# The low parts of a transform's operands on one engine, and two products of an MLP ahead of a layer

## The chip, the cores and the metric

The kernel runs on one core of a Trainium2 chip. The metric is the device time of one execution in microseconds (us). One launch takes eight float32 inputs and writes a float32 output of 2048 x 576.

## The reference

A token-mixing Fourier layer and an MLP read the same normalised input, and both are added to the input:

```python
xn = layernorm(x)                       # x: 2048 x 576
a  = xn @ dft_hid_re.T                  # first transform, along the 576 columns
b  = xn @ dft_hid_im.T
y  = dft_seq_re @ a - dft_seq_im @ b    # second transform, along the 2048 rows
h  = relu(xn @ w1)                      # w1: 576 x 4608
out = x + y + h @ w2                    # w2: 4608 x 576
```

The DFT matrices are inputs like the weights; no structure of theirs is used.

## The kernel before

**Numbers.** Every matrix product is made with float16 operands that come in two parts: a high part (the value rounded to float16) and a low part (the value less its high part, again in float16). A product is the sum of high x high, high x low and low x high. To make a split operand costs one rounding and one subtraction; the products themselves are blocked two by two and follow a scheme with seven multiplications, so that sums and differences of blocks are split as well.

**The engines' parts.** TensorE (PE in the profile) makes the products in float32 accumulators (PSUM). ScalarE (ACT) rounds and copies, VectorE (DVE) subtracts, adds and reduces, GpSimd (POOL) reduces over partitions, issues the DMAs that add results to a buffer `spill` in DRAM, and makes some subtractions. SyncE (SP) issues the loads and the transposing DMAs. Each engine works through its own instructions in the order in which the program lists them; the lists are written out by hand, as sequences of steps with names. `pinned(f)` issues the instructions of a step behind all that were issued before on PE, ACT and DVE.

**Stages.** The MLP runs over 9 blocks b of 512 columns of `w1`, and in each over 4 groups g of 512 rows of x; a step n is one pair (b, g). In step n, TensorE makes layer 1 of (b, g) and, between its parts, the seven products (0 to 6) of layer 2 of the step before, `mlp2_mm` (line L703). Layer 1 of block 0 is made by `mlp1_step` (L392 for the full depth of 128, L417 for the remaining 64 columns). The results of the products are read out of PSUM by `mlp2_out`: products 0, 2, 3 and 6 by a copy on ScalarE (L718), products 1, 4 and 5 by an add on VectorE (L722). Two PSUM buffers serve the products, so a product that starts a new buffer waits for an earlier read-out.

In block 0 the input is still being prepared. For group 3, four tiles are normalised (L306, L307), split (L313, L316) and transposed by four DMAs that SyncE issues (`transposes_dma`, L330). The first part of layer 1 of step 3, (0, 3), is the first reader of what these four transposes write. The steps 3 to 7 follow the sequence written out in the diff: `layer` is a part of layer 1, `m` a product of layer 2, `out2` its read-out, `slot`, `t_sum`, `then` and `count` are chores and read-outs that stand at that place when there are any (in step 3 the places "a" and "b" and the two `then`s hold nothing).

**The first transform.** It follows the MLP, in 8 steps s (two for each group). In a step TensorE makes seven products P1 to P7 for each half e of the columns (`dproduct`, L1429), in accumulators U0, U1, V and W. `take` reads them out, to a buffer X in float32: as copies on ScalarE (L1465) or as adds on VectorE (L1463). The take "u" for e = 1 is an add on VectorE that reads U1. Behind it `drests` (L1445), short matmuls over the remaining 64 columns, write U0, U1, W and V anew, so they can only begin when these have been read.

`convert(s, k)` makes, from a finished half of X, the seven split operands that the second transform reads. Its pieces have names:

- h1, h2, h3a, h3b: high parts, on ScalarE (L1476)
- l1, l2, l3a, l3b: low parts, `tensor_tensor` subtractions at L1480; l3a and l3b cover 128 x 576 each, and so does l1; l2 covers 128 x 288
- t13, t2, t4: differences of blocks in place, on VectorE (L1484, L1492, L1493)

`convert(s, 1)` ("one") is begun in step s itself and ended in step s + 1, where its end has the name "old"; `convert(s, 0)` ("two") is wholly made in step s + 1, under the name "late". So each of the steps 1 to 7 has two l3a and two l3b. Their order within a step, from the hand-written sequence, with the takes between them:

```python
("old", "t4"), ("old", "l3b"), ("old", "h3a"), ("late", "l1"), ("late", "h2"), (P5, 0), ("old", "l3a"), ("late", "l2"),
...
("c22", None), (P6, 1), ("r21", 1), ("late", "h3b"), ("late", "h3a"), (P7, 0), ("u", 0),
("late", "l3b"), (P3, 0), (P7, 1), ("u", 1), ("late", "l3a"), ("m", 0),
(P3, 1), ("rest", 0), ("w", None), ...
```

Before the change, l3a and l3b go to GpSimd in the steps 1 to 6 and to VectorE in step 7: a list `late_r` is empty until step 7 begins.

**The second transform** (`product`, L1644, with read-out at L1652) follows, with the split operands of `cre` and `cim` made on ScalarE and VectorE (L229, L230).

Of the kernel before, what the change touches and what calls it, by code (L numbers as in the profile page):

```python
# [54 lines left out]
def kernel(  # L55
# [17 lines left out]
    nc = tc.nc  # L73
# [611 lines left out]
    def mlp2(b, g, n):  # L685
        mlp2_mm(b, g, n)
        mlp2_out(b, g, n)
# [362 lines left out]
    def pinned(f, *a):  # L1050

        traced = nc.cur_bb.bb.instructions
        n = len(traced)
        with ExitStack() as s:
            for i in tails.values():
                s.enter_context(tc.issue_after(i))
            f(*a)
        for i in traced[n:]:
            if i.engine in ENGINES:
                tails[i.engine] = i  # L1060
# [187 lines left out]
    for n in range(2, len(steps)):  # L1248
        b, g = steps[n]
# [13 lines left out]
        if b >= BB:  # L1263
# [4 lines left out]
            then = lambda k: pinned(pend.pop(k)) if k in pend else None  # L1268
            m = lambda q: pinned(mlp2_mm, pb, pg, q)
            out2 = lambda q: pinned(mlp2_out, pb, pg, q)  # L1270
            slot = lambda k: [pinned(f) for f in chores.pop((g, k), ())]
            count = lambda q: pinned(passes.pop(0)) if passes else None
            more = lambda q: g % 2 and count(q)
            t_sum = lambda q: n == BB * NG and pinned(next, tq, None)
# [16 lines left out]
        if n > 2:  # L1291
            if n == 3:
                pend = {}
            psn = []
            m = lambda q: pinned(mlp2_mm, pb, pg, q)
            out2 = lambda q: pinned(mlp2_out, pb, pg, q)
            then = lambda k: pinned(pend.pop(k)) if k in pend else None
            layer = lambda i: pinned(mlp1_step, b, g, i, psn)
            now = lambda ks: [pinned(pairs[-1][k]) for k in ks.split()]
            pair = lambda i: pairs.append(pair_out(b, g, i, *psn[2 * i : 2 * i + 2]))  # L1300
            slot = lambda k: [pinned(f) for f in chores.pop((g, k), ())] if b else [pinned(work) for _ in range(WORK[k])]
            t_sum = lambda q: [pinned(next, tq, None) for _ in range(int(TS[n][q]))]
            count = lambda q: pinned(passes.pop(0)) if (n, q) > (6, 0) else None
            pairs = []
            for do, q in (
                (layer, 0), (then, "out6"), (slot, "a"), (then, "hS"), (t_sum, 0), (then, "lS"), (m, 0), (out2, 0),
                (slot, "b"), (t_sum, 1), (m, 1), (out2, 1), (slot, "c"), (t_sum, 2), (layer, 1), (count, 0),
                (t_sum, 3), (pair, 0), (now, "r hA hB lA s3 s1 s2 lB s4"), (m, 2), (out2, 2), (t_sum, 4),
                (m, 3), (out2, 3), (now, "hS"), (t_sum, 5), (now, "lS"), (slot, "d"), (layer, 2), (slot, "e"), (t_sum, 6),
                (m, 4), (out2, 4), (slot, "f"), (t_sum, 7), (m, 5), (out2, 5), (slot, "g"), (t_sum, 8), (count, 1),  # L1310
                (layer, 3), (pair, 1), (now, "r hA hB lA s3 s1 s2 lB s4"), (t_sum, 9), (slot, "h"), (m, 6),
            ):
                do(q)
            pend = {k: pairs[1][k] for k in ("hS", "lS")}
            pend["out6"] = lambda b=pb, g=pg: mlp2_out(b, g, 6)
            continue
# [147 lines left out]
        else:  # L1464
            order["da"] = nc.scalar.activation(dst, src, AF.Copy, scale=SCALE).ins  # L1465

    late_r = []

    def convert(s, k):

        g, c = divmod(s, 2)
        x, r = X[s % 2][:, k], R[g * TG + 2 * k + c]
        tt = nc.vector.tensor_tensor

        def hi(a, b):
            nc.scalar.activation(r[:, 0, a], x[:, b], AF.Copy)  # L1476

        def lo(a, b):
            tt = (nc.gpsimd if a.start > 2 and not late_r else nc.vector).tensor_tensor
            tt(r[:, 1, a], x[:, b], r[:, 0, a], ALU.subtract)  # L1480

        def t13():
            pair = x.rearrange("p (a b) e -> p a b e", b=2)[:, :, 0]
            tt(pair, x[:, 2:], pair, ALU.subtract)  # L1484

        return {
            "h1": lambda: hi(slice(0, 2), slice(0, 2)),
            "l1": lambda: lo(slice(0, 2), slice(0, 2)),
            "h2": lambda: hi(slice(2, 3), slice(3, 4)),
            "l2": lambda: lo(slice(2, 3), slice(3, 4)),  # L1490
            "t13": t13,
            "t2": lambda: tt(x[:, 3], x[:, 3], x[:, 0], ALU.subtract),  # L1492
            "t4": lambda: tt(x[:, 1], x[:, 1], x[:, 3], ALU.subtract),  # L1493
            "h3b": lambda: hi(slice(5, 7), slice(2, 4)),
            "l3b": lambda: lo(slice(5, 7), slice(2, 4)),
            "h3a": lambda: hi(slice(3, 5), slice(0, 2)),
            "l3a": lambda: lo(slice(3, 5), slice(0, 2)),
        }
# [52 lines left out]
    for s in range(NS):  # L1551
        lows = [(s, 0, P4), (s, 0, P3), (s, 1, P4), (s, 1, P3)]
        lows += [(s, e, P2) for e in range(2)]
        if s + 1 < NS:
            lows += [(s + 1, e, P5) for e in range(2)]
        end = s == NS - 1
        if end:
            late_r.append(True)
        one, two = convert(s, 1), convert(s, 0)
        if s == 0:  # L1560
            seq = (
                (P1, 0), ("pend", "out6"), ("pend", "s42"), ("c11", 0), ("pend", "hi1"), ("pend", "lo0"),
                 ("mlp", 0), ("pend", "lo1"),
                (P5, 0), ("c22", 0), ("mlp", 1), ("tail", 0), (P6, 0), ("r21", 0), ("mlp", 2), ("tail", 0),
                (P7, 0), ("u", 0), ("mlp", 3), ("tail", 0), (P3, 0), ("mlp", 4), ("tail", 0),
                (P1, 1), ("c11", 1), ("mlp", 5), ("tail", 0), (P5, 1), ("c22", 1), ("mlp", 6),
                (P6, 1), ("r21", 1), (P4, 0), (P7, 1), ("u", 1), ("open", 0), (P3, 1), ("rest", 0),
                ("c21", 0), ("w", None),
                ("one", "h1"), ("one", "l1"), ("one", "h2"), ("one", "l2"),
                (P4, 1), ("c21", 1), ("one", "t13"), ("one", "t2"),  # L1570
                (P2, 0), (P2, 1), ("v", None), ("one", "h3b"),
            )
        else:
            seq = (
                (P1, 0), ("c11", 0), ("late", "h1"), (P1, 1), ("c11", 1), ("old", "t4"), ("old", "l3b"),
                ("old", "h3a"), ("late", "l1"), ("late", "h2"), (P5, 0), ("old", "l3a"), ("late", "l2"),
                ("late", "t13"), (P6, 0), ("r21", 0), ("late", "t2"), ("late", "t4"), (P5, 1),
                ("c22", None), (P6, 1), ("r21", 1), ("late", "h3b"), ("late", "h3a"), (P7, 0), ("u", 0),
                ("late", "l3b"), (P3, 0), (P7, 1), ("u", 1), ("late", "l3a"), ("m", 0),
                (P3, 1), ("rest", 0), ("w", None), ("m", 1), ("m", 2), (P4, 0), ("c21", 0), ("one", "h1"),  # L1580
                ("one", "l1"), (P4, 1), ("c21", 1), ("one", "h2"), ("one", "l2"), ("one", "t13"), ("one", "t2"),
                (P2, 0), (P2, 1), ("v", None), ("one", "h3b"),
            )
        for what, e in seq:
            if what in ("old", "late", "one"):
                d = {"old": old, "late": late, "one": one}[what]
                if e in d and not (end and what == "one"):
                    pinned(d.pop(e))
            elif what == "pend":
                pinned(pend.pop(e))  # L1590
            elif what == "mlp":
                pinned(lambda: mlp2(*steps[-1], e))
            elif what == "tail":
                pinned(tail.pop(0))
            elif what == "open":
                ps2.release()
                psv = accumulators(("V", 2), ("W1", 2), side="left")
            elif what == "rest":
                pinned(lambda: drests(lows))
            elif what == "m":  # L1600
                if end:
                    pinned((lambda: operand(0), lambda: operand(1), lambda: addends(2))[e])
            elif isinstance(what, str):
                pinned(lambda: take(s, what, e))
            else:
                pinned(lambda: dproduct(s, e, what))
        old, late = one, two
        if s == 0:
            load_c(0, [0])
        if s == 3:  # L1610
            pinned(lambda: next(scale_c, None))
        if s == 5:
            load_c(0, [2, 3, 1])
# [47 lines left out]
    for n, (p, kh) in enumerate(units):  # L1661
# [7 lines left out]
        for i, (q, rq, first, row, col) in enumerate(PRODUCTS):  # L1669
            m = n * 7 + i  # L1670
# [73 lines left out]
```

## Time and profile before

| what | us |
|---|---|
| median of 3 runs | 1223.71 (1222.91 to 1224.64) |
| the profiled execution | 1222.8 |
| its span in the profile | 1221.0 |
| TensorE busy | 1208.1 |
| VectorE busy | 1005.6 |
| ScalarE busy | 720.2 |
| GpSimd busy | 192.5 |

The span runs from the first to the last instruction of the program; the execution's own time has 1.8 us around it. Busy times overlap, engine by engine. A row of the timeline has its start, its length, the engine, the line, the operation, what it writes and reads, and how many instructions in a row it stands for; in brackets the idle time of the engine before it and who ended that.

### The profile page before, as it was taken

How to read it: one execution, taken by the hardware profiler on the slowest of the kernel's cores; microseconds unless marked ns; L12 is line 12 of the kernel's file. 1: busy time of each engine (PE TensorE's matmuls, PEld its weight loads, DVE VectorE, ACT ScalarE, POOL GpSimd, SP SyncE). 2: the span in 40 equal slices, each digit the busy share in tenths (PEclk: the TensorE clock that was granted, in tenths of full speed). 3: DMA queues.
4: the chain of work that ended last, by engine and by line, in shares of the span. 5: the costliest groups of instructions: out<-in, count | busy, mean ns of one | idle time of the engine just before them, and what ended most of it. 6: DMA issues, size and time to landing. Idle time of an engine off the chain costs nothing.

```text
span 1221.0 us, 24573 instructions
## 1 busy us (share of the span) xinstructions
PE 1208.1 (99%) x10173; PEld 956.4 (78%) x10173; DVE 1005.6 (82%) x1623; ACT 720.2 (59%) x1077; POOL 192.5 (16%) x229
## 2 busy tenths in 40 slices
PE   8999999999999999999999999999999999999998
PEld 7656567888888888888888888877777777777776
DVE  9998998887797788788877977667898978787875
ACT  5646565866676776767666767555644433433342
POOL 2431211111121211111111211144300000000000
PEclk9999999999999999999999999999999999999999
DMA  9995645767666676667676667520165254534320
GB/s 320 210 156 87 104 73 136 154 136 162 157 133 168 132 180 127 142 151 153 136 164 157 126 160 158 94 30 1 62 205 179 72 185 137 177 108 147 100 89 20
DMA packets 84063, 164.64 MB, mean 135 GB/s; under 512 B 22640, under 2 KB 43632, under 8 KB 83952
## 3 DMA queue, kind: packets, MB, share of 16 engines
q1 hardware_dynamic: 61168, 120.61, 31.7%
q0 software_dynamic: 22784, 42.48, 25.0%
q8 instruction: 79, 1.29, 0.4%
q14 instruction: 32, 0.26, 0.1%
HBM read 110.76 MB, written 53.08 MB: 134 GB/s over the span
## 4 chain that ended last, share of the span: by engine, by line
PE 93%; DVE 5%; ACT 1%; issue 1%; DMA 0%; SPq 0%; ACTq 0%; DVEq 0%
PE p L703 30%; PE p L1644 27%; PE bank L608 23%; PE p L392 5%; PE U L1429 3%; PE W L1429 2%; PE bank L627 1%; PE V L1429 1%; DVE st L255 1%; DVE arena L230 0%; DMA arena<-in_x_dram 0%; DVE arena L306 0%; ACT arena L1476 0%; DVE arena L468 0%; DVE arena L451 0%
## 5 line engine op out<-in xcount | busy, mean ns | idle before, releaser
L703 PE MATMUL p<-arena 128*128 128x288 f16 x3024 | 398.9, 286 | 1.3 <-DVE arena L722 1.2
L703 PEld LDWEIGHTS <-arena 128*128 128x128 f16 x3024 | 295.9, 98 | 77.3 <-issue 1.9
L1644 PE MATMUL p<-arena 128*128 128x288 f16 x2688 | 329.4, 286 | 0.0
L1644 PEld LDWEIGHTS <-arena 128*128 128x128 f16 x2688 | 263.0, 98 | 66.3
L608 PE MATMUL bank<-arena 128*128 128x256 f16 x2580 | 304.8, 273 | 0.0
L608 PEld LDWEIGHTS <-arena 128*128 128x128 f16 x2580 | 250.1, 98 | 37.5 <-issue 5.9
L229 ACT ACTIVATE arena<-arena,sc_c 128x1024 f16<-128x1024 f32 x112 | 128.7, 1150 | 189.7 <-PE p L1644 137.4
L725 POOL DMA_DIRECT2D spill<-arena x144 | 128.5, 903 | 551.3 <-DVE arena L722 456.9
L230 DVE SCALAR_TENSOR_TENSOR arena<-arena,sc_c 128x1024 f16<-128x1024 f32 x112 | 143.4, 1281 | 29.6 <-ACT arena L229 25.8
L718 ACT ACTIVATE arena<-p,c_ub 128x576 f32<-128x576 f32 x144 | 105.8, 737 | 44.9 <-PE p L703 40.8
L230 DVE SCALAR_TENSOR_TENSOR arena<-arena,c_sw 128x640 f16<-128x640 f32 (+2 forms) x118 | 96.1, 849 | 31.0 <-ACT arena L229 30.9
L722 DVE SCALAR_TENSOR_TENSOR arena<-p,c_ub,arena 128x576 f32<-128x576 f32 x108 | 87.8, 814 | 20.8 <-PE p L703 19.3
L392 PE MATMUL p<-arena 128*128 128x128 f16 (+1 forms) x680 | 98.5, 300 | 3.9 <-issue 2.0
L636 DVE TENSOR_TENSOR arena<-bank,arena 128x512 f32<-128x512 f32 x84 | 57.9, 689 | 53.4 <-PE bank L608 52.2
L633 ACT ACTIVATE arena<-bank 128x512 f32<-128x512 f32 x112 | 66.5, 593 | 52.6 <-PE bank L608 52.5
L229 ACT ACTIVATE arena<-arena,c_sw 128x640 f16<-128x640 f32 (+2 forms) x118 | 88.7, 795 | 14.8 <-DVE c_sw L827 8.6
L1429 PEld LDWEIGHTS <-arena 128*128 128x128 f16 x738 | 71.6, 98 | 20.1 <-issue 2.4
L392 PEld LDWEIGHTS <-arena 128*128 128x128 f16 x680 | 52.2, 98 | 42.6 <-issue 6.1
L639 ACT ACTIVATE arena<-arena 128x512 f16<-128x512 f32 x84 | 53.0, 631 | 50.6 <-DVE arena L636 49.7
L1652 DVE SCALAR_TENSOR_TENSOR arena<-p,us_c,arena 128x288 f32<-128x288 f32 x112 | 57.5, 514 | 26.9 <-PE p L1644 26.6
L1227 ACT ACTIVATE arena<-arena 128x1024 f32<-128x1024 f32 x64 | 67.1, 1049 | 6.4 <-DMA arena<-in_cim_dram 5.0
L649 DVE TENSOR_TENSOR arena<-arena 128x1024 f16<-128x1024 f32 x56 | 68.2, 1217 | 0.3 <-ACT arena L645 0.3
(154 smaller groups left out, 1074.7 us busy)
## 6 DMA issues: line engine op xcount, KB each, us to landing
spill<-arena POOLq DMA_DIRECT2D x144, 288.0 KB, 5.2
arena<-in_cre_dram SPq DMA_DIRECT2D x64, 512.0 KB, 4.6
arena<-in_cim_dram SPq DMA_DIRECT2D x64, 512.0 KB, 4.8
arena<-in_w_dram SPq DMA_DIRECT2D x17, 640.0 KB, 6.1
arena<-in_w_dram SPq DMA_DIRECT2D x18, 576.0 KB, 3.8
arena<-spill SPq DMA_DIRECT2D x40, 144.0 KB, 2.2
arena<-in_x_dram SPq DMA_DIRECT2D x16, 288.0 KB, 6.7
spill<-in_x_dram SPq DMA_DIRECT2D x16, 288.0 KB, 5.9
```

The source lines that it names most:

```text
L229: nc.scalar.activation(hi, src, AF.Copy, scale=s).ins,
L230: nc.vector.scalar_tensor_tensor(lo, src, s, hi, ALU.mult, ALU.subtract).ins,
L392: order["m1"] = nc.tensor.matmul(ps[:, cols], w1s[b, i // 2][:, hl, i % 2 * KT + k], xT[g][:, kx, cols], start=(start and n == 0), stop=(s ...
L608: nc.tensor.matmul(ps[:, i], l, r, start=first and i == m == 0, stop=m == len(todo) - 1, skip_group_check=not first or i > 0,)
L649: order["lo"] = nc.vector.tensor_tensor(lo, stage[:, 1 + 2 * i :][:, :2], hi, ALU.subtract).ins
L703: order["pe"] = nc.tensor.matmul(ps[:, c], h[:, x, qa, c * P : (c + 1) * P], w[:, y, qb], start=first and i == 0 and j == 0, stop=i == NQ ...
L718: freed(nc.scalar.activation(o, ps, AF.Copy, scale=us[b]))
L722: add = nc.vector.scalar_tensor_tensor(o, ps, us[b], o, ALU.mult, ALU.add)
L725: nc.gpsimd.dma_start(spill[g, row, col], o, accum_op=ALU.add)
L1227: nc.scalar.activation(f, f, AF.Abs, scale=2.0**-10, accum_out=sums_c[:, n, q : q + 1])
L1429: nc.tensor.matmul(ps, l, r, start=first and m == 0, stop=m == len(todo) - 1, skip_group_check=not first,)
L1644: nc.tensor.matmul(ps, w[:, a, k], r[:, c, RQ[rq]], start=first and k == 0 and j == 0, stop=k == HK - 1 and j == 2, skip_group_check=not f ...
```

## The change

There are two parts.

In step 3, the last step of block 0, the products 0 and 1 of layer 2 of step 2, with their read-outs, come ahead of the first part of layer 1; in the later steps the order stays as it was.

In the first transform, the subtractions l3a and l3b go to VectorE in all steps, at the same places of the sequence. GpSimd has no arithmetic in this stage any more. Their number and sizes stay the same: 24 subtractions of 128 x 576 change engines, and nothing else changes place in that stage.

```diff
+            first = [(layer, 0), (then, "out6"), (slot, "a"), (then, "hS"), (t_sum, 0), (then, "lS")]
+            last = [(m, 0), (out2, 0), (slot, "b"), (t_sum, 1), (m, 1), (out2, 1)]
             for do, q in (
-                (layer, 0), (then, "out6"), (slot, "a"), (then, "hS"), (t_sum, 0), (then, "lS"), (m, 0), (out2, 0),
-                (slot, "b"), (t_sum, 1), (m, 1), (out2, 1), (slot, "c"), (t_sum, 2), (layer, 1), (count, 0),
+                *(first + last if n > 3 else last + first),
+                (slot, "c"), (t_sum, 2), (layer, 1), (count, 0),
                 (t_sum, 3), (pair, 0), (now, "r hA hB lA s3 s1 s2 lB s4"), (m, 2), (out2, 2), (t_sum, 4),
...
-    late_r = []
 
     def convert(s, k):
...
         def lo(a, b):
-            tt = (nc.gpsimd if a.start > 2 and not late_r else nc.vector).tensor_tensor
             tt(r[:, 1, a], x[:, b], r[:, 0, a], ALU.subtract)
...
         end = s == NS - 1
-        if end:
-            late_r.append(True)
         one, two = convert(s, 1), convert(s, 0)
```

Since the program is listed engine by engine, the read-outs of the two products move too: on ScalarE the copy of product 0 now stands ahead of four roundings of `w1` (L229), on VectorE the add of product 1 ahead of the four subtractions that belong to them (L230). The order on SyncE is the same; on GpSimd only the 24 subtractions are gone.

## The prediction

> **What bounds the kernel now.** I read the page first, for the busy engine and the chain that ended last, then TensorE's waits, then the two places that the change touches.
>
> ```profile
> span 1221.0 us, 24573 instructions
> ...
> PE 1208.1 (99%) x10173; PEld 956.4 (78%) x10173; DVE 1005.6 (82%) x1623; ACT 720.2 (59%) x1077; POOL 192.5 (16%) x229
> ...
> PEclk9999999999999999999999999999999999999999
> ...
> PE 93%; DVE 5%; ACT 1%; issue 1%; DMA 0%; SPq 0%; ACTq 0%; DVEq 0%
> ```
>
> TensorE is busy 1208.1 of 1221.0 us, its granted clock is full in every slice, and 93% of the chain is its own. So no engine time is to be had but TensorE's idle time, 12.9 us in all; whatever the change does to VectorE, ScalarE or GpSimd counts only where TensorE waits for it. Its waits, line by line:
>
> ```profile
> PE p L392 <- issue: 2.0, 1, 2.0
> PE p L703 <- DVE arena L722: 1.2, 2, 0.8
> ...
> PE U L1445 <- DVE arena L1463: 0.6, 1, 0.6
> PE U L1429 <- ACT arena L1465: 0.3, 1, 0.3
> ```
>
> Of the rows I show the ones that matter here: the first is the largest of all, and lies at the start of step 3; the last two are the only ones in the first transform. The rows left out, and the second one here, lie before step 3 by the timeline, in the kernel's beginning, which does not change. Between step 3 and the transform, and behind it, TensorE waits for nothing.
>
> **Part one: the two products ahead of the layer.** The chain of waits, in order of time, around the start of step 3:
>
> ```profile
> 72.56 7.35 PE p L703 x60
> 79.92 2.05 issue
> 81.96 2.97 PE p L392 x13
> ```
>
> Products 2 to 6 of the step before end at 79.92, then TensorE stands for 2.05 us, then layer 1 begins. "issue" says that the view found no releaser; the transposing DMAs are the likely one, for layer 1 of group 3 reads what they write:
>
> ```profile
> 74.96 2.73 SPq L330 DMA_TRANSPOSE arena<-arena  x1
> ...
> DMA to landing us min/median/max: 3.1/3.6/6.9
> ```
>
> The last of them is taken up at 74.96; the slowest takes 6.9 us to land, and 74.96 + 6.9 = 81.86, 0.1 before the first matmul of the layer. Now the products' own needs. Product 0 needs the buffer that product 5 leaves, product 1 the one that product 6 leaves:
>
> ```profile
> 78.48 0.82 DVE L722 SCALAR_TENSOR_TENSOR arena<-p,c_ub,arena 128x576 f32<-128x576 f32 x1 [0.57 <-PE p L703]
> 79.95 0.74 ACT L718 ACTIVATE arena<-p,c_ub 128x576 f32<-128x576 f32 x1 [1.78 <-PE p L703]
> ...
> 83.69 2.99 ACT L229 ACTIVATE arena<-arena,c_sw 128x640 f16<-128x640 f32 x4 [2.99 <-DVE c_sw L171]
> ...
> 84.55 3.27 DVE L230 SCALAR_TENSOR_TENSOR arena<-arena,c_sw 128x640 f16<-128x640 f32 x4
> ...
> 88.71 3.69 DVE L551 TENSOR_TENSOR arena<-arena 128x512 f32<-128x512 f16 x6
> 93.98 1.39 ACT L718 ACTIVATE arena<-p,c_ub 128x576 f32<-128x576 f32 x2
> 96.90 1.27 PE L703 MATMUL p<-arena 128*128 128x288 f16 x9
> ```
>
> Product 5 is read out at 78.48 + 0.82 = 79.30, before TensorE is free at 79.92. In the chain 60 matmuls of five products take 7.35, so one product takes 1.47: product 1 starts at 81.39, and product 6 is read out at 79.95 + 0.74 = 80.69. Both run without a wait; they end at 79.92 + 2.94 = 82.86, and the transposes have landed 1.0 earlier. So the 2.05 us go whole, and what is late next is nothing within 0.7 us. Bounds: 0, if a later wait takes it back, and 2.2, because 2.05 is counted from the modelled end of the last matmul and not from when the next could have begun. I take 2.05.
>
> The two read-outs change places. ScalarE's copy of product 0 (ready at 81.4) comes ahead of four roundings that began at 83.69 after an idle time of 2.99, so it falls into idle time. VectorE's add of product 1 comes ahead of four subtractions that began at 84.55 and pushes them by its 0.8 us; behind them it no longer stands, so the next work, the sums of x at 88.71 (L551), begins when it did. The loads behind the four subtractions, on SyncE, go out up to 0.8 later, for weights that are read a step later.
>
> Does a lead of 2 us survive? TensorE now runs 2 us earlier against everything that did not move. The thinnest place I find: ScalarE's copies at 93.98 stand behind work that waits for the sums of x, which stay where they are. Product 4 needs the first of the two copies, read out by about 93.98 + 0.7 = 94.7, and would now start at 96.90 - 2.05 = 94.85. That is enough by 0.15 or a little more, since the copies also move up where TensorE releases them. Farther on VectorE must keep up:
>
> ```profile
> 82.00:204.00 122.00, 122.00 (x800) 76.35 (x801) 110.96 (x221) 73.31 (x121) 21.91 (x27) 1.00 0.57 104
> ```
>
> From 82 to 204 us it is busy 110.96 of 122.00. The 11 us of idle time are waits for the other engines, so its work moves up with theirs. Over the whole span its share is lower (82%, the page). I count nothing lost; 0.5 is my estimate of what the place before product 4 may take, a copy of 0.7 less the 0.15.
>
> **Part two: 24 subtractions on VectorE.** The stretches are the steps 1, 2, 4 and 7 of the first transform, cut where TensorE comes out of the short matmuls:
>
> ```profile
> core 0: us, PE busy (x) PEld busy (x) DVE busy (x) ACT busy (x) POOL busy (x), PEclk, DMA share, GB/s
> 800.40:812.40 12.00, 11.38 (x95) 8.65 (x93) 9.65 (x15) 6.74 (x15) 4.26 (x3) 1.00 0.11 19
> 812.40:824.38 11.98, 11.98 (x103) 9.23 (x101) 9.00 (x15) 7.00 (x15) 5.73 (x6) 1.00 0.01 1
> 836.35:848.78 12.43, 12.16 (x103) 9.25 (x101) 9.99 (x19) 6.89 (x15) 4.65 (x4) 1.00 0.01 1
> 872.72:884.57 11.85, 11.85 (x100) 9.13 (x99) 10.27 (x19) 8.10 (x17) 1.11 (x1) 1.00 0.09 26
> ```
>
> The undisturbed step 2 takes 11.98, step 4 takes 12.43: 0.45 more. Step 1 takes 12.00 with 7 matmuls fewer, by the order of the program (the trace has 95 against 103, some records are missing); at 11.98 / 103 = 0.116 each they are worth 0.8, so step 1 loses about 0.85. The waits show 0.6 and 0.3 for the same two places, counted from modelled ends. So 1.3 us can be won at most, 0.9 by the waits alone. What ended these waits is VectorE late, and the timeline shows why it is late:
>
> ```profile
> L1480 POOL TENSOR_TENSOR arena<-arena 128x576 f16<-128x576 f32 x24 | 32.0, 1348 | 43.2 <-ACT arena L1476 43.2
> ...
> 807.03 3.31 POOL L1480 TENSOR_TENSOR arena<-arena 128x576 f16<-128x576 f32 x2 [8.39 <-ACT arena L1476]
> 807.36 1.84 DVE L1484 TENSOR_TENSOR arena<-arena 128x576 f32<-128x576 f32 x1
> 809.23 1.42 DVE L1492 TENSOR_TENSOR arena<-arena 128x288 f32<-128x288 f32 x1
> ...
> 820.94 0.74 DVE L1484 TENSOR_TENSOR arena<-arena 128x576 f32<-128x576 f32 x1
> 821.72 0.46 DVE L1492 TENSOR_TENSOR arena<-arena 128x288 f32<-128x288 f32 x1
> ...
> 814.49 1.13 DVE L1480 TENSOR_TENSOR arena<-arena 128x576 f16<-128x576 f32 x2 [1.40 <-ACT arena L1476]
> 818.40 2.62 DVE L1480 TENSOR_TENSOR arena<-arena 128x576 f16<-128x576 f32 x2 [0.59 <-ACT arena L1476]
> ...
> 841.59 1.25 DVE L175 TENSOR_SCALAR pw_c<-half 128x16 int32<-128x16 int32 x1
> ```
>
> The same `tensor_tensor` (L1484) takes 1.84 while GpSimd subtracts and 0.74 while it does not; L1492 takes 1.42 against 0.46; the pair l1 and l2 takes 2.62 against 1.13. In step 4 a `tensor_scalar` on 16 columns takes 1.25. In step 1 this makes VectorE 1.84 + 1.42 - 0.74 - 0.46 = 2.06 later ahead of the add that the short matmuls wait for, in the steps like step 2 2.62 - 1.13 = 1.49, which they have hidden so far.
>
> [...]
>
> The price: each of the 24 took 1348 ns on GpSimd; on VectorE there is a step that already is the new one, step 7:
>
> ```profile
> 878.05 2.67 DVE L1480 TENSOR_TENSOR arena<-arena 128x576 f16<-128x576 f32 x4
> ...
> 882.65 0.75 DVE L1480 TENSOR_TENSOR arena<-arena 128x576 f16<-128x576 f32 x1
> 883.35 0.46 DVE L1463 SCALAR_TENSOR_TENSOR arena<-U,arena 128x288 f32<-128x288 f32 x1
> ...
> 884.23 0.28 PE L1445 MATMUL U<-arena 64*128 64x288 f16 x1
> ```
>
> Four in a row take 2.67 (three of 576 columns and one of 288), a single one 0.75, 0.67 with the overlap. So VectorE takes 24 x 0.67 = 16 us more and gets some 8 to 10 back from the lengthened ones; per step 4 x 0.67 = 2.7 more and 1.5 less, 10.2 of 11.97, which is what the row of step 7 has (10.27). And step 7 ran without a wait: the add on U1, with l3b before it, ends at 883.35 + 0.46 = 883.81, the short matmul that overwrites U1 starts at 884.23. The margin is 0.42 per step. I expect the steps 1 to 6 to run like step 7. In step 1 VectorE gains 2.06 and gets two subtractions (1.35) ahead of the late add, and one (0.67) between the two adds, which it can have since it comes early by then: the 0.85 go. In step 4 four tiny operations for a scale come on top (0.4 after the long one is short); they use up the margin, so I count 0.4 of the 0.45. GpSimd's side costs nothing: it has nothing else to do there.
>
> **The sum.** 2.05 + 0.85 + 0.4 = 3.3. The profiled execution becomes 1222.8 - 3.3 = 1219.5; the median of the runs lies 0.9 above it, so 1220.4 is forecast, 0.27% less.
>
> **The rivals.** (a) Only part one pays: the step after the change keeps its waits because VectorE, though free of GpSimd, is just as late by its own new work (it gets 2.0 in step 1, about what it saves). For it: in step 1 savings and price are equal within 0.1 if all three subtractions count. Against it: the third stands behind the first add, and in step 7 all fits. 1223.7 - 2.05 = 1221.7.
>
> (b) The lead of part one is used up, at the copies at 93.98 or by a load that lands when it did; part two pays. Against it: TensorE waits nowhere between 82 and 800, and the one thin place takes tenths. 1223.7 - 1.25 = 1222.5.
>
> (c) The other side: VectorE becomes the bound of the transform. If its lengthening is not GpSimd's doing, or comes back by another door, a step costs what step 7 does plus 1.49, less the margin of 0.42, so 1.07 in each of the steps 2 to 6: 5.4. With 2.05 won, 1223.7 + 5.4 - 2.05 = 1227.0. It decides from the point where VectorE's turn is 0.42 longer than in step 7. For it: VectorE is the busiest engine beside TensorE, and in step 4 its margin is all but gone. Against it: not one `tensor_tensor` in step 7 is longer than 0.76, with the same work in the same order. [...]
>
> (d) Neither pays, by (a) and (b) together: 1223.7, no change.
>
> **How the numbers follow.** Forecast 0.66; (a) 0.13; (b) 0.06; (c) 0.09; (d) 0.06. The likeliest case is 3.3 us with bounds of 2.5 (0.5 lost at the copies, 0.3 more kept in the transform) and 3.6 (2.2 + 0.9 + 0.45), so 1220.1 to 1221.2, and the runs before differ by 0.9 either way, which makes 1219.2 at the low end. Upwards the range has to take in (a) and (b): 1222.6. What lies outside, (c) and (d), has 0.15. A measurement of this kernel tells from no change about 0.2%, 2.4 us: the forecast's case is beyond it, with a little chance of falling short of it, (a), (b) and (d) are within it, (c) is beyond it on the other side. So faster 0.63 (0.66 less 0.03), same 0.28, slower 0.09.
>
> **What would show it.** Part one: in the chain of waits the 2.05 of issue is gone, and 24 matmuls of L703 lead over into L392 without a gap; the copies of ScalarE before product 4 end before TensorE comes to it. Part two: no `tensor_tensor` of L1480, L1484 or L1492 in the transform over 0.76, GpSimd's busy time down by 32 to 160, VectorE's up by 6 to 8; steps 2 to 6 at 11.97, step 1 at about 11.1, and no wait of L1445 or L1429. I am wrong on part one if a wait of about 2 us stands elsewhere before 210 us, on part two if L1445 waits for L1463 in each step, or if VectorE's subtractions stay long with GpSimd idle.

## The result, and the profile after

| | median us | range, runs |
|---|---|---|
| before | 1224.26 | 1222.91 to 1225.64, 6 |
| changed | 1220.24 | 1219.70 to 1220.61, 6 |
| ratio | 0.9967 | 95% interval 0.9954 to 0.9979 |

The changed kernel is faster by 0.33%, about 4.0 us; 1220.4 was forecast. Its profiled execution took 1220.53 us. The page, the first rows of TensorE's waits, and the chain of waits around step 3, all of the changed kernel:

```profile
span 1218.5 us, 24554 instructions
...
PE 1208.0 (99%) x10173; PEld 956.6 (79%) x10173; DVE 1011.0 (83%) x1647; ACT 720.6 (59%) x1077; POOL 160.3 (13%) x205
...
PE 95%; DVE 4%; ACT 1%; DMA 0%; issue 0%; SPq 0%; ACTq 0%; DVEq 0%
```
```profile
PE p L703 <- DVE arena L722: 1.2, 2, 0.8
PE p L392 <- ACT arena L347: 1.1, 1, 1.1
```
```profile
70.54 3.02 PE p L392 x14
73.56 10.29 PE p L703 x84
83.85 2.81 PE p L392 x13
```

TensorE's work is the same (1208.0 us). The wait of 2.0 at L392 and the two of the transform are gone from the list, and in the chain 84 matmuls of the products (seven times 12) lead over into the layer without a gap. VectorE has 5.4 us more, GpSimd 32.2 less.

The execution falls into three stretches with clear cuts: from the first layer-2 product to the first product of the transform, the transform, and from the first product of the second transform to the end. The table by windows, before and after; the second column is the length, then the busy times (TensorE, weight loads, VectorE, ScalarE, GpSimd):

```profile
45.28:780.49 735.21, 731.88 (x6077) 577.21 (x6076) 612.21 (x1065) 497.09 (x783) 136.56 (x166) 1.00 0.67 142
780.49:888.01 107.52, 106.63 (x886) 82.27 (x884) 79.68 (x124) 62.28 (x126) 37.05 (x30) 1.00 0.22 45
888.01:1221.00 332.99, 329.44 (x2690) 262.92 (x2687) 272.46 (x301) 130.49 (x118) 0.00 (x0) 1.00 0.41 129
```
```profile
46.31:779.28 732.97, 731.69 (x6077) 577.30 (x6076) 611.68 (x1065) 497.50 (x783) 136.43 (x166) 1.00 0.66 143
779.28:885.50 106.22, 106.22 (x886) 82.18 (x884) 85.35 (x148) 62.43 (x126) 5.00 (x6) 1.00 0.21 45
885.50:1218.50 333.00, 329.44 (x2690) 262.92 (x2687) 272.56 (x301) 130.37 (x118) 0.00 (x0) 1.00 0.39 129
```

The first stretch, with part one in it, lost 735.21 - 732.97 = 2.24 us; the transform 1.30, and there TensorE is busy for 106.22 of 106.22: nothing more is to be won in it by removing waits. The end is the same. Together that is 3.54, but the span fell by 2.5 only: this execution's first product began 1.03 later, at 46.31 against 45.28. Nothing was changed there; the chain of waits shows why, first before, then after:

```profile
2.12 4.79 DMA arena<-in_x_dram
```
```profile
2.12 5.80 DMA arena<-in_x_dram
```

The first load of x, on which the whole beginning hangs, took 1.01 longer to land.

### The profile page after: what moved, and what is told of

The parts are those of the page before. It is cut to its first block, busy times and chain, and to the rows that moved or that the text cites. A ratio compares the mean times of both kernels' runs of the same rounds, so it can differ in the third digit from the quotient of the medians.

```text
span 1218.5 us, 24554 instructions
## 1 busy us (share of the span) xinstructions
PE 1208.0 (99%) x10173; PEld 956.6 (79%) x10173; DVE 1011.0 (83%) x1647; ACT 720.6 (59%) x1077; POOL 160.3 (13%) x205
## 4 chain that ended last, share of the span: by engine, by line
PE 95%; DVE 4%; ACT 1%; DMA 0%; issue 0%; SPq 0%; ACTq 0%; DVEq 0%
PE p L703 30%; PE p L1642 27%; PE bank L608 23%; PE p L392 5%; PE U L1431 4%; PE W L1431 2%; PE bank L627 1%; PE V L1431 1%; DVE st L255 1%; DVE arena L230 0%; DMA arena<-in_x_dram 0%; DVE arena L306 0%; DVE arena L468 0%; DVE arena L451 0%; DVE arena L837 0%
## 5 line engine op out<-in xcount | busy, mean ns | idle before, releaser
L229 ACT ACTIVATE arena<-arena,sc_c 128x1024 f16<-128x1024 f32 x112 | 128.6, 1149 | 189.8 <-PE p L1642 137.8
L230 DVE SCALAR_TENSOR_TENSOR arena<-arena,sc_c 128x1024 f16<-128x1024 f32 x112 | 143.4, 1281 | 29.4 <-ACT arena L229 26.7
L230 DVE SCALAR_TENSOR_TENSOR arena<-arena,c_sw 128x640 f16<-128x640 f32 (+2 forms) x118 | 96.0, 849 | 31.0 <-ACT arena L229 31.0
L392 PE MATMUL p<-arena 128*128 128x128 f16 (+1 forms) x680 | 98.5, 300 | 1.8 <-ACT arena L347 1.1
L229 ACT ACTIVATE arena<-arena,c_sw 128x640 f16<-128x640 f32 (+2 forms) x118 | 88.7, 794 | 15.9 <-DVE c_sw L827 9.8
L392 PEld LDWEIGHTS <-arena 128*128 128x128 f16 x680 | 52.3, 98 | 40.3 <-issue 3.8
L1650 DVE SCALAR_TENSOR_TENSOR arena<-p,us_c,arena 128x288 f32<-128x288 f32 x112 | 57.5, 513 | 27.0 <-PE p L1642 26.6
```

The lines of the kernel that those rows point to most:

```text
L229: nc.scalar.activation(hi, src, AF.Copy, scale=s).ins,
L230: nc.vector.scalar_tensor_tensor(lo, src, s, hi, ALU.mult, ALU.subtract).ins,
L392: order["m1"] = nc.tensor.matmul(ps[:, cols], w1s[b, i // 2][:, hl, i % 2 * KT + k], xT[g][:, kx, cols], start=(start and n == 0), stop=(s ...
```

## The experiments

All medians are compared with the kernel before, timed on the same chip in the same job; "full clock" means executions whose mean granted TensorE clock is listed as 1.000.

**The kernel before, profiled again.** Its run times come in two heaps, so two more of its executions were profiled on one chip, with no edit.

> The kernel before, unchanged, looked at again. Kernels whose step 3 begins with the layer (the kernel before, part two alone) spread over 3 us from run to run, those with a product ahead of it over 1 us. If the spread comes from TensorE's idle 2 us at step 3, an execution of about 1225 us shows there either a longer wait (3 to 4 us, the transposes landing later) or a lower granted clock behind it (2 us lost over some us of matmuls at half speed); everything else up to 1222.8 is the same. If it comes from elsewhere, the extra 2 us stand at another place, before 60 us or in block 1.

> As look 1, another execution: at 1222.5 to 1223.6 the trace of before comes again (wait 2.0 to 2.3, full clock), at 1224 to 1226 the extra 2 us are to be seen at the start of step 3, as a longer wait or as a lower clock.

One took 1224.75, the other 1223.15. The chain of waits of the first, then of the second:

```profile
80.16 2.06 issue
82.22 4.65 PE p L392 x13
86.88 2.94 PE p L703 x24
```
```profile
80.30 2.11 issue
82.41 2.97 PE p L392 x13
```

The wait is the same, but in the first execution the granted clock falls to 0.50 behind it: the same 13 matmuls take 4.65 instead of 2.97, 1.7 us more. The clock was at half for 3.41 us (the row from 82.59 to 86.00 below), and half of that is the 1.7 us. The execution that the prediction was read from was one without this dip. How often it comes is seen in the times. Of the 75 executions of the kernel before in the jobs of these experiments, 35 had full clock and took 1223.20 us in the mean; the 40 with less took 1225.06, 1.9 more. A listed clock below 1.000 is only a rough sign of this dip: the first execution, listed with 0.997, has a second dip at 17.74, in the kernel's beginning, and in the profile of the changed kernel the clock is at half for the last 0.42 us of the span, from 1218.08 on, when TensorE has finished (at 1214.96).

The traces say more about when the clock changed. From its first change to its last it is 1215.15 us in the profile of before and 1211.73 in that of the changed kernel, 356 and 355 times 3.413. The dip behind step 3 lasted 3.41, and one in the kernel with an unread write (the last run) 6.83, twice that. Here are two intervals of such a grid around the wait, counted from the first change, in the first execution, then in the second (a table by windows; the last three columns are granted clock, DMA share, GB/s):

```profile
79.18:82.59 3.41, 1.35 (x10) 0.77 (x9) 3.41 (x5) 0.74 (x1) 2.52 (x3) 1.00 1.27 137
82.59:86.00 3.41, 3.41 (x10) 1.22 (x8) 2.94 (x12) 2.07 (x3) 0.70 (x2) 0.50 1.18 188
```
```profile
78.61:82.02 3.41, 1.69 (x14) 1.11 (x12) 3.15 (x4) 0.74 (x1) 2.79 (x3) 1.00 1.30 133
82.02:85.43 3.41, 3.02 (x15) 1.49 (x16) 2.94 (x12) 1.36 (x2) 1.15 (x3) 1.00 1.22 197
```

In the first execution the whole wait falls into one interval, and the next one runs at half clock; in the second it is cut into 1.72 and 0.39, and the clock stays full. In the profile of the changed kernel TensorE was idle for 3.14 of the 3.41 us before 1218.08, and there the clock fell too. But the dip at 17.74 came behind two waits of 0.4 and 1.1, 1.53 us in all, so the length of the idle time isn't the whole of it. For the wait of 2.05 it seems to matter where it lies on the grid. As an estimate from these numbers, (3.41 - 2.05) / 3.41, or 40% of the executions, would have the dip, if the wait must lie in one interval as a whole, and 59%, if any part longer than the 1.72 of the second execution is enough.

**Part one alone.** The kernel before with the new order in step 3:

```diff
+            first = [(layer, 0), (then, "out6"), (slot, "a"), (then, "hS"), (t_sum, 0), (then, "lS")]
+            last = [(m, 0), (out2, 0), (slot, "b"), (t_sum, 1), (m, 1), (out2, 1)]
...
+                *(first + last if n > 3 else last + first),
...
```

> Part one alone; the 24 subtractions stay on GpSimd. If the 2.05 us of TensorE's idle time at step 3 is the landing of the transposes and nothing behind it takes the lead back, this kernel is 2.1 us faster than the one before (2.0 to 2.2), the wait of L392 for issue is gone, and the two waits of the first transform (0.6 and 0.3) stand as before. If the lead is lost at the copies ahead of product 4 or in block 1, it is under 1 us faster, with a new wait of L703 before 210 us.

1220.87 (1220.50 to 1221.65, 8 runs) against 1224.67 (24 runs), ratio 0.9973 [0.9963, 0.9983]; by means 3.4 us. Its chain and the waits left in the transform:

```profile
72.81 10.29 PE p L703 x84
83.10 2.86 PE p L392 x13
```
```profile
PE U L1447 <- DVE arena L1465: 0.6, 1, 0.6
PE U L1431 <- ACT arena L1467: 0.3, 1, 0.3
```

The wait goes and the transform keeps its own (107.56 us long). All 8 executions had full clock. Against the executions of before at full clock in the same job (mean 1223.32, 9 of them) the gain is 2.4; the other 15 (mean 1224.87) make the remaining 1.0 by 15/24 x 1.55. So part one is worth the wait and, in about half the executions, the dip behind it. The cover is thinner than it looked: in this profile the last transpose landed at 82.90, 0.2 before the layer.

**One product ahead instead of two.** As before, with only product 0 and its read-out first:

```diff
+                *(first + last if n > 3 else last[:2] + first + last[2:]),
```

> Of part one only half: product 0 and its read-out ahead of the layer, product 1 behind it; the subtractions on GpSimd as before. If the layer waits for the landing of the last transpose, one product of 1.47 us covers that much of 2.05: 1.5 us faster, and a wait of 0.6 (0.4 to 0.7) for issue is left before the layer. If the layer waited for something that follows the end of the products before it (a buffer, a read-out), the whole wait of 2 us would follow product 0 and nothing would be gained.

1222.05 (1221.59 to 1222.71, 11 runs), ratio 0.9981 [0.9973, 0.9990]. The chain of waits:

```profile
72.84 8.82 PE p L703 x72
81.66 0.67 issue
82.33 2.97 PE p L392 x13
```

One product (1.47) leaves 0.67 of the wait, and the layer begins at 82.33, 0.09 after the last transpose lands. So what ended the wait is the landing of the transposes, and the second product is needed. A wait of 0.67 brought no dip: the 5 executions with less than full clock took 1221.95 in the mean, the 6 with it 1222.19. The profiled one is listed with 0.999, but the 13 matmuls behind its wait took 2.97, as at full clock.

**The wait filled with useless work.** The kernel before, with 32 matmuls on zeros in TensorE's queue ahead of the layer of step 3, whose sum nobody reads: TensorE is kept busy, nothing is moved.

```diff
...
+            if (b, g) == (0, 3):
+                for _ in range(32):
+                    nc.tensor.matmul(ps[0][:, :P], idle, idle, start=True, stop=True)
```

> The kernel before, in its old order, with 32 matmuls of zeros (128 x 128 by 128 columns, 0.056 each, 1.8 us) in TensorE's queue ahead of the layer of step 3, into the bank that the layer starts anew; they add nothing to the result. The wait for the transposes stays, the array only isn't idle in it. If about half of the executions of the kernel before lose 1.7 us to a halved clock behind that wait, these are gone: 1222.8 to 1223.6 with a spread of about 1 us, a median 1 to 2 us under that of the kernel before. If the idle time isn't what lowers the clock, the executions of 1224 to 1226 stay, and the median is that of the kernel before.

1223.75 (1223.16 to 1224.63, 11 runs) against 1223.86 (1222.59 to 1226.58, 21 runs), ratio 0.9998 [0.9989, 1.0006]. The chain of waits:

```profile
72.67 7.35 PE p L706 x60
80.03 1.79 PE p L425 x32
81.81 0.76 issue
82.57 2.97 PE p L392 x13
```

The upper heap is gone, as expected: 7 of the 21 executions of before lie above 1224.63, none of these 11. But the median didn't fall. By the profile the transposes landed later, so that work and wait together last 2.55 us instead of 2.05, and the stretch up to the transform took 735.69 instead of 735.21. At full clock the kernel is 0.45 slower than the one before (1223.81, 9 runs, against 1223.36, 13 runs), which fits that 0.5 but is hardly more than the noise of the two means. Why the landing came later isn't known.

**Part two alone.** The kernel before without `late_r`, so that all l3a and l3b are on VectorE:

```diff
-    late_r = []
...
-            tt = (nc.gpsimd if a.start > 2 and not late_r else nc.vector).tensor_tensor
...
-        if end:
-            late_r.append(True)
```

> Part two alone; step 3 begins with the layer as before. If VectorE was late in steps 1 and 4 of the transform because GpSimd held it up, both waits there go and the kernel is 1.3 us faster (0.9 to 1.4), with the 2.05 us at step 3 left. If VectorE's new work takes the place of the old hold-ups, it is within 0.3 us of the kernel before, with L1445's wait still there; if VectorE is the bound, it is slower, by up to 5 us, and each step shows the wait.

1224.25 (1221.99 to 1225.16, 11 runs), ratio 0.9998 [0.9989, 1.0007]; its mean is 0.5 under that of before, and 0.56 at full clock (1222.76, 3 runs, against 1223.32). Its transform took 106.21 us, as in the changed kernel: the 1.3 are won there, and about half of it is missing in the times. With three executions at full clock the 0.56 is uncertain by about 0.6.

**GpSimd repeats the subtractions.** The changed kernel, where GpSimd makes every l3a and l3b again, behind VectorE's own and to the same place:

```diff
             tt(r[:, 1, a], x[:, b], r[:, 0, a], ALU.subtract)
+            if a.start > 2:
+                nc.gpsimd.tensor_tensor(r[:, 1, a], x[:, b], r[:, 0, a], ALU.subtract)
```

> The changed kernel, and after each l3a and l3b on VectorE GpSimd makes the same subtraction once more, to the same place (32 in all, the result is the same). VectorE has not one instruction more than in the changed kernel. If a subtraction on GpSimd holds up a two-input subtraction of VectorE, l1 and l2 and the later l3a are lengthened again by 0.4 to 1.2 each, VectorE loses 1.4 or more of a margin of 0.4 in each of the steps 1 to 7, and the kernel is 5 to 9 us slower than the changed one, with L1447 waiting for L1465 in each step. If the long ones had another cause, all stays at 0.75 and 0.45 and the time within 0.5 us of the changed kernel's.

**GpSimd only writes.** The changed kernel with three memsets on GpSimd, which read nothing, ahead of each l3a and l3b, on the place that VectorE then writes:

```diff
+            if a.start > 2:
+                for _ in range(3):
+                    nc.gpsimd.memset(r[:, 1, a], 0.0)
             tt(r[:, 1, a], x[:, b], r[:, 0, a], ALU.subtract)
```

> The changed kernel, and ahead of each l3a and l3b GpSimd writes zeros three times to the place that the subtraction then writes (96 memsets of 128 x 576, most of them in a row from about 800 us on). GpSimd is busy in the first steps of the transform, but reads nothing. If reading is what holds VectorE up, the subtractions stay at 0.75 and 0.45 and the time stays within 0.5 us of the changed kernel's. If any work of GpSimd does it, the subtractions in steps 1 to 3 are lengthened and TensorE waits there.

The repeating kernel took 1238.30 us (4 runs), ratio 1.0111 [1.0096, 1.0126], 18 us over the changed kernel; every theory had it lower (5 to 9). In its profile 16.9 of them lie in the transform, which took 123.1. The writing one took 1220.28 (1219.69 to 1220.80, 5 runs), ratio 0.9966 [0.9953, 0.9979], like the changed kernel. TensorE's waits in the transform, of the repeating, then of the writing kernel:

```profile
PE U L1447 <- DVE arena L1465: 12.1, 14, 1.5
```
```profile
PE U L1447 <- DVE arena L1465: 0.2, 1, 0.2
```

And VectorE's groups in the transform, by shape, of the repeating kernel and of the changed one:

```profile
L1480 DVE TENSOR_TENSOR arena<-arena 128x576 f16<-128x576 f32 x42 | 44.0, 1064 | 6.6 <-ACT arena L1477 5.9
L1486 DVE TENSOR_TENSOR arena<-arena 128x576 f32<-128x576 f32 x14 | 18.1, 1290 | 0.0
```
```profile
L1480 DVE TENSOR_TENSOR arena<-arena 128x576 f16<-128x576 f32 x42 | 31.0, 753 | 10.1 <-ACT arena L1477 9.4
L1484 DVE TENSOR_TENSOR arena<-arena 128x576 f32<-128x576 f32 x14 | 10.5, 751 | 0.0
L1492 DVE TENSOR_TENSOR arena<-arena 128x288 f32<-128x288 f32 x14 | 6.4, 458 | 0.5
...
L175 DVE TENSOR_SCALAR pw_c<-half 128x16 int32<-128x16 int32 x1 | 0.2, 167 | 0.0
```

VectorE's own work is the same in both; with GpSimd subtracting beside it the mean of one goes from 753 to 1064 ns and from 751 to 1290. None of VectorE's idle time in this stage is put down to GpSimd, so it isn't waiting for the repeated results; its instructions themselves take longer. Busy GpSimd that only writes leaves these subtractions at 754 and 751 ns, though 48 memsets, 26.6 us of work, run beside them between 800 and 880 us. So GpSimd's subtractions, which read and compute, lengthened VectorE's, and its memsets, which only write, did not; whether it is the reading alone these two runs don't tell. The price of one more such GpSimd instruction is higher than all theories had it: a step went from 11.97 to 14.0.

One instruction of VectorE took longer beside memsets. In the writing kernel, first GpSimd, then VectorE:

```profile
835.12 3.63 POOL L1482 MEMSET arena<- 128x576 f16 x6 [1.31 <-PE U L1431]
```
```profile
838.25 0.53 DVE L170 TENSOR_SCALAR half<-top 128x16 f32<-128x16 f32 x1
```

This `tensor_scalar` takes 0.16 in the changed kernel. Here it ends with the last memset, at 838.78 and 838.75, and the interval between the short matmuls is 0.4 longer there, with the wait of 0.2 shown above.

**How much room VectorE has.** The changed kernel with an idle reduction on VectorE between l3b and the add on U1, once in each of the steps 1 to 7, over 288 or over 1024 columns:

```diff
-                ("late", "l3b"), (P3, 0), (P7, 1), ("u", 1), ("late", "l3a"), ("m", 0),
+                ("late", "l3b"), (P3, 0), (P7, 1), ("delay", 0), ("u", 1), ("late", "l3a"), ("m", 0),
```

> The changed kernel with one more VectorE instruction in each of the steps 1 to 7, between l3b and the add on U1: a reduction over 288 columns, 0.44 long by the row of the reduction over 640 (0.81), 0.36 net of the overlap. The margin of that add was read as 0.42. So this is just covered: within 0.5 us of the changed kernel, at most 0.1 a step.

> The same with a reduction over 1024 columns, 1.21 long, 1.13 net. If the margin is 0.4, each of the seven steps is 0.7 longer, 5.0 us in all (4.5 to 5.6), with a wait of L1447 for L1465 of 0.7 in each. If VectorE had room elsewhere in the step that the add could draw on, it is under 2 us.

With 288 columns (445 ns) the kernel took 1220.89 (1220.48 to 1221.49, 6 runs), and only one wait of 0.2 appears; with 1024 columns (1211 ns) 1225.81 (1225.51 to 1226.22, 10 runs), with this wait in each of the seven steps:

```profile
PE U L1447 <- DVE arena L1465: 4.4, 7, 0.9
```

Counted from the end of one group of short matmuls to the end of the next, four of the seven intervals became 0.73 or 0.74 longer, so 1.21 - 0.74 = 0.47 of each reduction was free there. The margin read from step 7 of the profile of before was 0.42. The other three, in steps 1, 2 and 4, became 0.95, 0.78 and 1.12 longer; in step 4 only 0.09 was free, as the prediction had it for the step with the four tiny operations.

**Part two on top of the filled wait.** The filled kernel with `late_r` taken out:

> The same fill, with part two of the change: what part two is worth with the spread of step 3 taken out. By the traces of single executions 1.3 us (0.86 in step 1 and 0.45 in step 4) less than the kernel with the fill alone, so about 1221.7 to 1222.2. If part two were worth what part two alone showed against the kernel before (0.0 to 0.5), it is that.

1223.20 (1222.34 to 1224.05, 11 runs), ratio 0.9992 [0.9983, 1.0001]; by means 0.74 under the filled kernel, 0.66 at full clock. Once more the transform took 106.21; in the profile of the filled kernel it was 107.21, so here 1.0 was to be won. By the mean spans at full clock (1221.94 and 1220.99) it arrives within the noise, and 0.29 is given back in the time outside the span. The profiled execution doesn't show this: it was the slowest of the 11, and 1.3 more than in the changed kernel's profile lies behind its last matmul.

**An unread write on GpSimd.** The last run asked whether the missing half goes with the build:

```diff
+    scr = const.tile([P, 1], F32, name="scr")
...
+            if a.start > 2:
+                nc.gpsimd.memset(scr, 0.0)
             tt(r[:, 1, a], x[:, b], r[:, 0, a], ALU.subtract)
```

> The changed kernel with one more GpSimd instruction ahead of each l3a and l3b: it sets one column of a scratch tile that nobody reads. Open is where 0.65 us of the 1.3 that the transform gives up in the traces went: the changed kernel, part two alone and the filled kernel with part two had 1.9 to 2.1 us of the execution outside the span and began layer 2 at 46.0 to 46.3 us, while the delays and the writing GpSimd, with the same subtractions on VectorE, had 1.7 to 1.8 and 45.3 to 45.8. Theory: that belongs to how a build is laid out in memory or loaded, not to the subtractions; then this kernel, whose transform should run as in the changed kernel (steps at 11.12 and 11.97 to 11.99), can fall on either side: with 1.78 outside the span and a median near 1219.6, or with 2.0 and 1220.2, and its median goes with the time outside the span. Rival: the subtractions on VectorE cost the 0.65 in the transform in executions that are not the profiled ones; then the median is 1220.2 whatever lies outside the span.

1222.98 (1221.92 to 1224.39, 10 runs), ratio 0.9993 [0.9984, 1.0003]: neither 1219.6 nor 1220.2. The edit didn't stay where it was meant. The 32 memsets, which depend on nothing, stood in a row at GpSimd's start, from 0.72 on; its timeline and one row of TensorE's waits:

```profile
0.72 4.94 POOL L1482 MEMSET scr<- 128x1 f32 x32 [0.29 <-POOLq L1734]
```
```profile
PE pt L336 <- POOL arena L313: 2.5, 1, 2.5
```

They hold GpSimd for 4.94 us, TensorE waits for GpSimd 2.5 in the beginning, the granted clock is at half for 6.83 us from 19.24 on, and layer 2 begins at 50.10. The transform took 106.22 again. So the run doesn't answer its question; it shows only that 2 to 3 us of this kernel hang on a beginning that no one meant to touch.

## Why the prediction was right, point by point

**What bounds the kernel** was read rightly: TensorE's busy time is the same to 0.1 us, and VectorE's 5.4 us more (6 to 8 were expected) cost nothing.

**Part one** has its mechanism and its cover as worked out: no gap before the layer, which now starts at 83.85, 1.0 after the last transpose has landed (82.86). The thin place held too. The timeline of the changed kernel there:

```profile
89.29 3.69 DVE L551 TENSOR_TENSOR arena<-arena 128x512 f32<-128x512 f16 x6
...
94.56 1.39 ACT L718 ACTIVATE arena<-p,c_ub 128x576 f32<-128x576 f32 x2
...
95.69 2.49 PE L703 MATMUL p<-arena 128*128 128x288 f16 x19
```

The first of the two copies ends near 94.56 + 0.69 = 95.25, the next product starts at 95.69: 0.44 to spare where at least 0.15 was expected. The term that was mis-sized is the 2.05. In executions at full clock it is 2.2 to 2.4; over all executions 3.4, for the dip of the clock behind the wait was missing. It couldn't be read from the one profile of before, but the times could have raised the question: they stood 0.9 above the profiled execution, which the prediction carried along as an offset to the changed kernel, too.

**Part two** came out step by step as said. From one group of short matmuls to the next, the seven intervals of before were 11.74, 12.22, 11.97, 12.40, 12.00, 11.97 and 11.98 us; after, they are 11.12, 11.97, 11.98, 11.97, 11.99, 11.97 and 11.98. The first two give 0.87 (0.85 predicted), the fourth 0.43 (0.4). No `tensor_tensor` of the three lines means more than 0.753, and the small `tensor_scalar` fell from 1.25 to 0.167. GpSimd's busy time fell by 32.2 to 160.3, as said. Rival (c) falls: in steps 2 to 6 VectorE's turn isn't longer than in step 7, and its price holds, for the long delay showed that VectorE is the bound as soon as its turn grows by more than 0.47, and in step 4 by more than 0.09.

**The sum** came so close by luck. In the forecast's own terms two misses cancel: the profiled execution, foreseen at 1219.5, took 1220.53, and the median of the runs lay 0.3 below it, not 0.9 above. The terms were off as well. In the two stretches 3.54 was won against 3.3. To this come 1.0 in the mean by the dips; but part two is worth 0.66 in the run times, not 1.25: changed kernel less part one alone, 1220.25 - 1220.91 at full clock (from two jobs), and 0.56 and 0.66 in the other two pairs. Each of these is uncertain by 0.4 to 0.6; that the whole 1.25 doesn't arrive is clear from the three together. About 0.25 of the 0.65 that is missing against the 1.3 of the profiles is seen in every execution. The time of an execution outside its span is 1.72 to 1.81 us for part one alone and 1.90 to 2.10 for the changed kernel; 1.72 to 1.84 for before and 1.89 to 2.12 for part two alone. The other 0.4 lies by subtraction in the span. In the two profiles only the beginning differs apart from the transform: the first load of x took 5.05 in that of part one alone, 5.80 in that of the changed kernel. In the seven profiles in which the chain shows this load, it takes 4.79 to 5.80, and layer 2 begins 38.35 to 38.43 after it has landed. Whether the new kernels load later by their build or by chance is open: there is one profile of each, and the two kernels with delays, with the same subtractions on VectorE, had 5.30 and 4.86, and 1.72 to 1.83 outside the span. So the rivals (a), (b) and (d) fall for what the change does in its two places, while in the run times part two is worth about half, for reasons that the profiles place outside both and that stay open.

## What to carry to other kernels

A wait of TensorE in a dense stream can cost more than its length (the 2.06 us here cost another 1.7 by the half clock behind them), and it can be hidden by independent products that stand just behind it in the program, if their buffers come free in time (84 matmuls without a gap here). When a kernel's times fall into two heaps, take a second profile before counting: the one at hand may lack a term. And where a step of the program already runs in the new way, as step 7 did here, it is the best price list for the change: duration, order and margin held to 0.05 us here, but for the step that has four operations more.

## What was not expected of the hardware

- A wait of 2.06 us was followed by 3.41 us at half clock in one execution and, at 2.11, by none in another. The first lay wholly in one interval of the grid of 3.413 us on which the clock changed, the second was cut by its edge into 1.72 and 0.39. A wait of 0.67 brought no slower heap.
- GpSimd's subtractions of 128 x 576 made VectorE's two-input operations of that size 1.4 to 1.7 times as long in the mean; memsets on the same buffers left them at 0.75, but a `tensor_scalar` on 16 columns took 0.53 beside them instead of 0.16.
- Builds that differ only in a late stage differ by about 0.25 us in the time outside the span (1.72 to 1.81 us for part one alone, 1.90 to 2.10 for the changed kernel); why isn't known.
